# A gated linear attention kernel with a convolution-gated MLP: state updates of 48 columns, transposes of 112 rows, and a rewritten later part of the order

## The chip, the core and the metric

The kernel runs on one core of a Trainium2 chip. A core has five instruction queues that run side by side: PE (TensorE, matrix products, with its weight loads listed as PEld), DVE (VectorE), ACT (ScalarE), POOL (GpSimd) and SP (SyncE, which here only issues DMAs). The metric is the device time of one execution in microseconds (us). Before the change it is 304.14 us, the median of three runs (304.11 to 306.39).

## What is computed

Four sequences (b) of 768 steps with eight heads of 48 dimensions go through a gated linear recurrence. Its output goes through an MLP whose hidden layer is gated by a convolution over three neighbouring steps.

```
for t in range(S):                                # 768 steps
    state = f[:, :, t, :, None] * state + k_t (outer) v_t     # 48 x 48 for each head
    y[:, :, t] = q_t @ state
x = y of all heads side by side                   # 4 x 768 x 384
h = relu(x @ w_in)                                # 384 -> 1024
gate = sigmoid(conv_w[0]*h[t-1] + conv_w[1]*h[t] + conv_w[2]*h[t+1])
out = (h * gate) @ w_out                          # 1024 -> 384
```

All inputs are fp32, and f is the sigmoid of `f_logit`.

## The kernel before, in words

**Attention.** A sequence is cut into 6 chunks of 128 steps, so there are 24 chunks, numbered n = 0 to 23; c = n mod 6 is the chunk's place in its sequence. Heads are handled in four pairs p, the two heads j = 0, 1 of a pair in partitions 0 to 47 and 64 to 111. For each chunk, cumulative decays give `fi` and `fd`, by which k (on DVE, `scaled_k`) and q (mostly on POOL, `scaled_q`) are multiplied. Then:

- `turned` transposes k into a PSUM tile `ptk` (4 transposes of 128 by 128), and ACT copies 48 of each 64 columns to `kp`.
- `scores` makes the products of k and q in the PSUM tile `pa` (one tile for all chunks), and DVE copies the causal part into `am` under a mask (COPY_PREDICATED). There are two `am` tiles, used in turn.
- `values` makes `py` (one PSUM buffer): first from `am` and v, then, where a state exists, from the state `st` and q. ACT and then DVE move `py` to `xT`, split into a rounded high part and a low part.
- `state` makes k^T v in a PSUM tile `pk`. DVE adds the old state to it, and POOL multiplies the sum by the chunk's total decay `ft_all` into the next `st`. `last_decay` copies that decay from `fd` on POOL. Chunks with c = 5 have no `turned` and no `state`, so there are 20 of each. `ptk` and `pk` share one PSUM buffer in turn.

For n < 9 the state products use weights of 64 columns (two column halves of the array beside each other), from n = 9 on weights of 32 columns (four beside each other). Each moves 64 columns of v: 48 of its own head and 16 more, in reversed 32-column blocks for j = 1. A state row is 4 pairs by 64 columns = 256 columns wide.

**MLP.** A unit u is half a sequence (384 steps). `hidden` makes for each of 8 blocks f a PSUM tile `ph` from 9 products of 384 columns (high and low parts of weights and inputs, fp32r). ACT applies relu, then ACT and DVE make the convolution, `gated` applies tanh and the gate. `result` splits this into `gh` (ACT) and `gl` (DVE), makes a tile `po` of 128 steps from 24 products of 384 columns, and stores it. `ph`, `po` and some early tiles share three PSUM buffers.

**The order.** Nothing is scheduled automatically. The text ORDER names steps, and each name runs one more piece of that step's generator: F, V, L, M load f, v, k, q; x, G, p make the decays; t is `last_decay`; K and Q scale k and q; k is `turned`, a `scores`, s `state`, y `values`; h, m, j are the MLP's first part and r its second; I, J, H, O, P, S are weights; z counts the decays that are not too small and b loads that count into a register of every engine, for a branch to a slow path that is not taken here. Each engine runs its own pieces in the order in which they are written, so an instruction that waits holds up all that is behind it on its engine.

## Time and profile before

| | before |
|---|---|
| median of 3 runs | 304.14 us |
| the profiled execution's own span | 303.3 us |
| PE busy | 294.2 us, 97% of the span |
| PEld busy | 273.5 us, 90% |
| DVE busy | 251.3 us, 83% |
| ACT busy | 220.5 us, 73% |
| POOL busy | 85.3 us, 28% |
| granted TensorE clock | 1.00 of full speed throughout |

The profile is one execution. It lists for each engine when it was busy, groups instructions by their line, says what ended the idle time before an instruction, and follows the chain of work that ended last: 75% of that chain is PE, 31% in `po` and 28% in `ph`. Matrix products are pipelined: the start of one to the start of the next is the time that it really takes, while the duration shown includes a fixed latency.

### The profile page before, as it was taken

The numbers are of one execution on the slowest core, as the hardware profiler recorded it, in microseconds if no ns is written. First come the engines' busy times: TensorE is split into PE (matmuls) and PEld (weight loads), VectorE is DVE, ScalarE is ACT, GpSimd is POOL, SyncE is SP. The second block draws the span as 40 slices with busy tenths as digits, with TensorE's granted clock in tenths as the row PEclk, the third lists the DMA queues.
The fourth block names the chain that finished last, engine by engine and source line by source line (L and its number), as shares of the span: only waits on it lengthen the run. The fifth ranks groups of instructions, "written<-read, shape, count | busy, mean of one in ns | idle before, by whom it ended". The sixth has DMA issues, their size and how long they took to land.

```text
span 303.3 us, 8894 instructions
## 1 busy us (share of the span) xinstructions
PE 294.2 (97%) x3747; PEld 273.5 (90%) x3747; DVE 251.3 (83%) x380; ACT 220.5 (73%) x422; POOL 85.3 (28%) x107
## 2 busy tenths in 40 slices
PE   7799989999999999999999999999999999999994
PEld 5678878988999999999998999999999999999994
DVE  4999999999999999977999999946893976479520
ACT  4999979989967996767976995665756544676521
POOL 5475894344503140300323410230305010000000
PEclk9999999999999999999999999999999999999999
DMA  7999951194025411627315130602012000000211
GB/s 230 396 385 391 403 191 39 56 333 135 2 72 161 101 59 61 220 72 224 102 37 166 64 124 2 195 2 84 3 30 89 2 28 26 28 1 2 79 54 55
DMA packets 19374, 35.67 MB, mean 118 GB/s; under 512 B 2156, under 2 KB 9092, under 8 KB 19332
## 3 DMA queue, kind: packets, MB, share of 16 engines
q1 hardware_dynamic: 19044, 34.69, 33.8%
q8 instruction: 30, 0.49, 0.7%
q10 hardware_dynamic: 288, 0.39, 0.4%
q14 instruction: 12, 0.10, 0.1%
HBM read 30.35 MB, written 4.72 MB: 116 GB/s over the span
## 4 chain that ended last, share of the span: by engine, by line
PE 75%; DVE 7%; POOL 3%; issue 1%; ACT 1%; POOLq 0%
PE po L507 31%; PE ph L454 28%; PE py L398 8%; PE pa L351 3%; PE ptk L330 2%; DVE g L466 2%; PE pk L376 2%; DVE g L464 2%; DVE g L475 1%; POOL st L386 1%; PE pa L345 1%; DVE am L358 1%; PE pk L371 1%; POOL q L324 1%; DVE gl L495 1%
## 5 line engine op out<-in xcount | busy, mean ns | idle before, releaser
L454 PE MATMUL ph<-xT,wih 128*128 128x384 f32 x384 | 99.6, 340 | 0.0
L454 PEld LDWEIGHTS ph<-xT,wih 128*128 128x128 f32 x384 | 68.3, 188 | 1.0 <-issue 0.2
L507 PE MATMUL po<-woh,gh 128*128 128x384 f32 x192 | 64.7, 337 | 0.0
L454 PE MATMUL ph<-xT,wil 128*128 128x384 f32 x192 | 64.3, 335 | 0.0
L507 PE MATMUL po<-wol,gh 128*128 128x384 f32 x192 | 64.2, 334 | 0.0
L507 PE MATMUL po<-woh,gl 128*128 128x384 f32 x192 | 64.2, 334 | 0.0
L464 DVE SCALAR_TENSOR_TENSOR g<-hb,cw,g 128x384 f32<-128x384 f32 (+1 forms) x64 | 42.2, 667 | 13.0 <-ACT g L462 12.9
L466 DVE SCALAR_TENSOR_TENSOR g<-hb,cw,g 128x384 f32<-128x384 f32 (+1 forms) x64 | 40.5, 649 | 0.7
L457 ACT ACTIVATE hb<-ph 128x384 f32<-128x384 f32 x64 | 30.7, 487 | 11.4 <-PE ph L454 10.8
L495 DVE TENSOR_TENSOR gl<-g,gh 128x1024 fp32r<-128x1024 f32 (+4 forms) x34 | 30.4, 908 | 9.6 <-ACT gh L493 9.6
L462 ACT ACTIVATE g<-hb,cw 128x384 f32<-128x384 f32 (+1 forms) x64 | 38.0, 614 | 0.3
L507 PEld LDWEIGHTS po<-woh,gh 128*128 128x128 f32 x192 | 36.0, 188 | 0.5 <-issue 0.2
L324 POOL TENSOR_TENSOR q<-q,fd 128x512 f32<-128x512 f32 x19 | 26.9, 1419 | 33.0 <-ACT fd L307 24.3
L507 PEld LDWEIGHTS po<-wol,gh 128*128 128x128 f32 x192 | 36.0, 188 | 0.0
L507 PEld LDWEIGHTS po<-woh,gl 128*128 128x128 f32 x192 | 36.0, 188 | 0.0
L454 PEld LDWEIGHTS ph<-xT,wil 128*128 128x128 f32 x192 | 36.0, 188 | 0.0
L493 ACT CAST gh<-g 128x1024 fp32r<-128x1024 f32 (+4 forms) x34 | 26.4, 800 | 12.7 <-PE po L507 8.8
L386 POOL TENSOR_TENSOR st<-st,ft_all 128x256 f32<-128x256 f32 x16 | 20.8, 1301 | 51.7 <-DVE st L384 51.7
L475 DVE SCALAR_TENSOR_TENSOR g<-g,hb 128x768 f32<-128x768 f32 (+1 forms) x32 | 30.1, 952 | 3.7 <-ACT g L473 3.7
L512 ACT COPY ob<-po 128x384 f32<-128x384 f32 x24 | 11.3, 474 | 29.7 <-PE po L507 27.1
L473 ACT ACTIVATE g<-g 128x768 f32<-128x768 f32 (+1 forms) x32 | 26.7, 846 | 3.9 <-DVE g L466 3.8
L312 POOL COPY ft_all<-fd 128x4 f32<-128x4 f32 x24 | 12.7, 537 | 56.5 <-ACT fd L307 56.5
(92 smaller groups left out, 453.9 us busy)
## 6 DMA issues: line engine op xcount, KB each, us to landing
k<-in_k_dram SPq DMA_DIRECT2D x24, 256.0 KB, 4.4
q<-in_q_dram SPq DMA_DIRECT2D x24, 256.0 KB, 4.3
v<-in_v_dram SPq DMA_DIRECT2D x24, 224.0 KB, 4.3
fb<-in_f_logit_dram SPq DMA_DIRECT2D x18, 256.0 KB, 4.3
out_dram<-ob SPq DMA_DIRECT2D x22, 192.0 KB, 1.9
wis<-in_moe_w_in_dram SPq DMA_DIRECT2D x6, 512.0 KB, 6.0
wos<-in_moe_w_out_dram SPq DMA_DIRECT2D x8, 384.0 KB, 5.6
fb<-in_f_logit_dram SPq DMA_DIRECT2D x6, 200.0 KB, 4.9
```

Of the source, the lines that this page charges most:

```text
L324: (nc.vector if n < QV else nc.gpsimd).tensor_tensor(raw["q", n], raw["q", n], fds[n][1], ALU.mult)
L398: nc.tensor.matmul(py[G * p:G * p + G, t, :], lhs, rhs, start=start, stop=stop)
L454: nc.tensor.matmul(ph, w, xts[b, hf][:, t, xl, :], start=(k == 0), stop=(k == 3 * KT - 1))
L457: nc.scalar.activation(hb[:, 2:HS + 2], ph, AF.Relu, scale=0.5)
L462: nc.scalar.activation(cv, hb[:, 1:n + 1], AF.Copy, scale=cw[:, 1, f:f + 1])
L464: nc.vector.scalar_tensor_tensor(cv, hb[:, 2:n + 2], cw[:, 2, f:f + 1], cv, ALU.mult, ALU.add)
L466: nc.vector.scalar_tensor_tensor(cv, hb[:, 0:n], cw[:, 0, f:f + 1], cv, ALU.mult, ALU.add)
L473: nc.scalar.activation(cv, cv, AF.Tanh)
L475: nc.vector.scalar_tensor_tensor(cv, cv, 1.0, h_b[:, fp:fp + 2, 1:n + 1], ALU.add, ALU.mult)
L493: nc.scalar.copy(hi, g[:, f:f + k])
L495: nc.vector.tensor_tensor(lo, g[:, f:f + k], hi.bitcast(F32), ALU.subtract)
L507: nc.tensor.matmul(po, g[:, f, :], w, start=(i == 0), stop=(i == 3 * NF - 1))
```

## The change

1. `state` moves 48 columns in place of 64, those of its own head alone, now contiguous. To pack them, a state row becomes 288 columns: head 0 of pair p in columns 64p to 64p + 47 of the upper partitions, head 1 in columns 64p + 48 to 64p + 95 of the lower ones. The slices that `values` loads as weights start at multiples of 64 bytes, as before.
2. Between these parts lie columns that hold leftovers of the transposes. They are made zero by the decay: `ft_all` has a value for each 16 columns (18 of them, and 2 spare), is zero to begin with, and is filled by two POOL copies of 64 partitions by 4 by 3 in place of one of 128 by 4.
3. `turned` transposes 112 rows of k (both heads' rows) in place of 128, so 112 columns come out.
4. `ptk` and `pk` become one tile `sk` that is kept throughout. It is cleared once by DVE.
5. ORDER: the first 386 of its 1403 names are the same, up to about 80 us of the execution before; behind them the same names are written in another sequence.

```diff
-    s_b = [wk.tile([P, NP, HP], F32, name=f"st{i}", bufs=1) for i in range(2)]
+    s_b = [wk.tile([P, WS], F32, name=f"st{i}", bufs=1) for i in range(2)]
+    sk = ps.tile([P, NP, P], F32, name="sk")
+    pk = sk.rearrange("p n t -> p (n t)")[:, :WS]
+    nc.vector.memset(pk, 0.0)
-    ft_all = const.tile([P, B, NC, NP], F32, name="ft_all")
-    nc.gpsimd.memset(ft_all, 1.0)
+    ft_all = const.tile([P, B, NC, NU + 2], F32, name="ft_all")
+    nc.gpsimd.memset(ft_all, 0.0)
...
-        (nc.scalar.copy if n >= TS else nc.gpsimd.tensor_copy)(ft_all[:, b, c, :], fds[n][1][:, :, P - 1])
+        for j in range(2):
+            r, i0 = slice(HP * j, HP * j + HP), D // GAP * j
+            nc.gpsimd.tensor_copy(ft_all[r, b, c, i0:i0 + NP * HP // GAP].rearrange("p (n i) -> p n i", n=NP)[:, :, :D // GAP],
+                                  fds[n][1][r, :, P - 1:].broadcast_to([HP, NP, D // GAP]))
...
-            nc.tensor.transpose(pt[:, p, :], raw["k", n][:, p, :], ident)
+            nc.tensor.transpose(sk[:, p, :W2], raw["k", n][:W2, p, :], ident[:W2, :W2])
...
-                vv = vt[:, p, D * j:D * j + HP].rearrange("p (i e) -> p i e", e=G)
-                vv = vv[:, ::-1] if j else vv
+                vv = vt[:, p, HP * j:HP * j + D]
+                for x in (0,) if n < NA else (0, G):
+                    o, w = HP * j + x, HP if n < NA else G
+                    nc.tensor.matmul(pk[o:o + w, HP * p + D * j:HP * p + D * j + D], kp[:, 2 * p + j, x:x + w], vv,
                                      start=True, stop=True)
...
-k13 y11 k13 y11 a12 k12 K14 m2.0 m2.6 p15 m2.1 y11 m2.3 r0.2 r0.3 m2.3 m2.1 r0.4 r0.4 y11 m2.5 m2.4 M15 r0.4 r0.4 r0.4
+p12 k13 y10 s10 G14 m2.1 Q12 t12 M14 r0.2 L15 r0.5 r0.5 j2.4 m2.0 r0.4 k12 a12 y11 a12 y11 k12 y11 r0.5 Q13 a13 j2.4
+y11 V12 s12 y12 r0.4 m2.1 m3.4 m3.4 s12 m2.7 m3.0 m3.4 x15 h3.4 m2.2 m3.4 m2.0 m2.2 m2.0 j2.0 y12 j2.0 G17 j2.6 m3.0
```

With it go W2 = 112, WS = 288 and NU = 18.

**PE, the state products of chunk 22, before.** The row of `pk` stands first in a group of fp32 products between two stretches of the MLP (`ph`, `po`); the numbers in the names are the chunk's.

```order
L454 MATMUL ph6_2_3463<-xT3_0_2812,wil2_0_456 128x384
L376 MATMUL pk22_3503<-v22_3498,kp0_79 32x64 x16
L398 MATMUL py22_3520<-am0_75,v22_3498 32x128 x16
L398 MATMUL py22_3520<-q22_3032,st0_77 32x128 x12
L351 MATMUL pa_81<-q23_3306,k23_2428 64x128 x2
```

**PE, the same chunk in the change.** The stretch is cut between the repeating rows of `pa`.

```order
L338 MATMUL sk_82<-ident_88,k22_2638 128x112 x4
L359 MATMUL pa_81<-q22_3244,k22_2638 64x128 x2
...
L401 MATMUL py21_3383<-am1_76,v21_2457 32x128 x16
L401 MATMUL py21_3383<-q21_2597,st1_78 32x128 x12
L359 MATMUL pa_81<-q23_3197,k23_2824 64x128 x2
...
L378 MATMUL sk_82<-v22_2818,kp0_79 32x48 x16
L401 MATMUL py22_3461<-am0_75,v22_2818 32x128 x16
L401 MATMUL py22_3461<-q22_3244,st0_77 32x128 x12
```

The products are 48 and 112 columns wide. Two chunks now stand in one group: `pa` of chunks 22 and 23 with only `py` of chunk 21 between them, and `py` of chunks 21 and 22 with `pa` and the state products between them. Chunks 12 and 13 stand in the same way. Counted to the end of the fast path, PE goes from the MLP's products to fp32 products 24 times before and 22 times in the change.

**DVE, around the mask copy of chunk 22 in the change.** COPY_PREDICATED reads `pa`; g5 and g6 are gates of MLP units 5 and 6.

```order
L499 TENSOR_TENSOR gl2_2_3252<-g4_2485,gh2_2_3251 128x8x127
L479 SCALAR_TENSOR_TENSOR g5_2874<-g5_2874,hb_110 128x770 x2
L329 TENSOR_TENSOR k23_2824<-k23_2824,fi23_3246 128x2x128 x2
L468 SCALAR_TENSOR_TENSOR g6_3353<-hb_110,cw_116,g6_3353 128x384
L366 COPY_PREDICATED am0_75<-mask1_101,pa_81 128x1024
L432 TENSOR_TENSOR xT3_1_3420<-py21_3383,xT3_1_3420 128x3x128
```

Two gates, a k and a piece of convolution stand ahead of the copy, and the low part of `py` of chunk 21 behind it.

**POOL, some 30 us into the program, before.**

```order
L386 TENSOR_TENSOR st1_78<-st1_78,ft_all_110 128x256
L181 TENSOR_SCALAR mswo3_541<-mswo3_541 128x384
L312 COPY ft_all_110<-fd3_346 128x4
L312 COPY ft_all_110<-fd4_490 128x4
L179 TENSOR_SCALAR mswo0_607<-wos0_409 128x384
```

**POOL, the same place in the change.**

```order
L388 TENSOR_TENSOR st1_78<-st1_78,ft_all_112 128x288
L187 TENSOR_SCALAR mswo3_539<-mswo3_539 128x384
L320 COPY ft_all_112<-fd3_348 64x4x3 x2
L320 COPY ft_all_112<-fd4_489 64x4x3 x2
L185 TENSOR_SCALAR mswo0_607<-wos0_410 128x384
```

Each decay copy has become two, and the state product is 288 columns wide; the order is the same here.

## Rows read from the trace of the kernel before

**Rows 1.** The page's first part: engine, busy us, share of the span, instructions

```profile
PE 294.2 (97%) x3747; PEld 273.5 (90%) x3747; DVE 251.3 (83%) x380; ACT 220.5 (73%) x422; POOL 85.3 (28%) x107
```

**Rows 2.** Busy time by stretches: length, each engine's busy us, PEclk, DMA share, GB/s

```profile
75.00:100.00 25.00, 25.00 (x285) 24.07 (x287) 24.93 (x39) 19.60 (x36) 7.63 (x10) 1.00 0.24 71
200.00:225.00 25.00, 25.00 (x290) 24.16 (x277) 18.63 (x29) 15.67 (x30) 4.59 (x6) 1.00 0.08 26
```

**Rows 3.** A wait of PE's products: for whom, us in total, times, longest

```profile
PE py L398 <- POOL st L386: 1.1, 1, 1.1
```

**Rows 4.** PE's products by line and shape: weights, moving columns, count, busy us, mean ns

```profile
L398 PE MATMUL py<-am,v 128*32 128x128 f32 x768 | 25.8, 275 | 0.4 <-DVE xT L428 0.3
L330 PE MATMUL ptk<-ident,k 128*128 128x128 f32 x80 | 12.8, 282 | 0.1
L376 PE MATMUL pk<-v,kp 128*32 128x64 f32 x384 | 7.7, 221 | 0.0
```

**Rows 5.** Weight loads by line and shape, the same columns

```profile
L454 PEld LDWEIGHTS ph<-xT,wil 128*128 128x128 f32 x192 | 36.0, 188 | 0.0
L330 PEld LDWEIGHTS ptk<-ident,k 128*128 128x128 f32 x80 | 8.9, 140 | 2.0 <-DVE st L384 0.3 <-DVE cw L248 0.2 <-ACT kp L333 0.2
L376 PEld LDWEIGHTS pk<-v,kp 128*32 128x32 f32 x384 | 6.3, 110 | 1.8 <-issue 1.5 <-ACT g L462 0.2
L371 PEld LDWEIGHTS pk<-v,kp 128*64 128x64 f32 x128 | 4.5, 137 | 0.9 <-issue 0.2 <-ACT wos L185 0.2
```

**Rows 6.** PE in order of time: start us, length us, product; three stretches

```profile
63.65 0.34 PE L454 MATMUL ph<-xT,wil 128*128 128x384 f32 x1
63.92 0.69 PE L371 MATMUL pk<-v,kp 128*64 128x64 f32 x16
...
176.17 0.66 PE L330 MATMUL ptk<-ident,k 128*128 128x128 f32 x4
176.58 0.59 PE L454 MATMUL ph<-xT,wih 128*128 128x384 f32 x2
...
244.44 0.65 PE L376 MATMUL pk<-v,kp 128*32 128x64 f32 x32
244.91 1.06 PE L398 MATMUL py<-am,v 128*32 128x128 f32 x32
...
246.50 0.90 PE L351 MATMUL pa<-q,k 48*64 48x128 f32 x32
...
247.33 0.44 PE L507 MATMUL po<-woh,gh 128*128 128x384 f32 x1
247.61 0.34 PE L507 MATMUL po<-wol,gh 128*128 128x384 f32 x1
247.78 0.35 PE L507 MATMUL po<-woh,gl 128*128 128x384 f32 x1
```

**Rows 7.** POOL's decay copies: count, ns min/median/max, first and last start

```profile
L312 POOL COPY ft_all<-fd x24: 183/513/1833, 12.5 to 219.4; 128x4 f32<-128x4 f32 x24
```

**Rows 8.** POOL and DVE in order of time, 35 to 46 us

```profile
35.35 0.68 DVE L317 TENSOR_TENSOR k<-k,fi 128x512 f32<-128x512 f32 x1
...
39.08 4.27 POOL L386 TENSOR_TENSOR st<-st,ft_all 128x256 f32<-128x256 f32 x1
...
42.87 1.27 DVE L355 COPY_PREDICATED am<-mask,pa 128x1024 f32<-128x1024 uint8 x1
...
44.90 1.80 DVE L317 TENSOR_TENSOR k<-k,fi 128x512 f32<-128x512 f32 x1
```

**Rows 9.** ACT and DVE behind the last rows of Rows 6

```profile
246.67 0.48 ACT L426 CAST xT<-py 128x384 fp32r<-128x384 f32 x1 [0.47 <-PE py L398]
...
248.36 0.55 DVE L428 TENSOR_TENSOR xT<-py,xT 128x384 fp32r<-128x384 f32 x1
...
249.35 1.32 DVE L358 COPY_PREDICATED am<-mask,pa 128x1024 f32<-128x1024 uint8 x1
```

**Rows 10.** DMA issues: size of one, median us from issue to landing

```profile
q<-in_q_dram SPq DMA_DIRECT2D x24, 256.0 KB, 4.3
```

More of the change, by code (lines that the diff above doesn't have):

```diff
@@ new lines @@
+m7.6 m7.6 m7.6 m7.7 r2.3 r2.3 m7.6 m7.6 m7.6 j7.6 m7.3 m7.3 j6.4 m7.4 m7.4 r2.3 m7.2 r2.2 m7.4 r2.3 m7.5 m7.5 m7.5
+r3.0 h7.4 j7.6 r2.4 r2.4 r2.4 r2.4 m7.2 m7.3 m7.2 m7.4 m7.1 m7.4 m7.5 m7.5 r2.3 r2.5 r3.0 r3.0 r3.0 r3.0 r3.0 j7.2
+m7.0 m7.1 m7.5 r3.1 m7.0 m7.0 r3.1 m7.4 m7.5 m7.1 m7.4 j7.2 j7.0 j7.0 r3.0 r3.2 r3.2 r3.2 r3.2 r3.2 r3.2 r3.2 j7.4
+r3.2 r3.2 r3.2 r3.2 r3.1 r3.1 r3.1 j7.4 r3.1 r3.2 r3.2 r3.2 r3.2 r3.3 r3.1 r3.1 r2.4 r3.2 r3.2 r3.2 r3.0 r3.2 r3.2
+r3.3 r3.3 r3.3 r3.4 r3.3 r3.4 r3.3 r3.5 r3.3 r3.4 r3.4 r3.4 z b r3.3 r3.2 r2.4 r3.5 r3.5 r3.2 r3.5 r3.5 r3.4 r3.4 r3.4
@@ L79 @@
+r3.5 r3.5 r3.5
 """
@@ L108, in gla_moe_kernel @@
     G = 32
+    W2 = HP + D
+    WS = HP * (NP - 1) + 2 * D
+    NU = WS // GAP
     WHOLE = False
@@ L327, in turned @@
     def turned(n):
-        pt = ps.tile([P, NP, P], F32, tag="s", name=f"ptk{n}", bufs=SB)
         for p in range(NP):
-            nc.tensor.transpose(pt[:, p, :], raw["k", n][:, p, :], ident)
+            nc.tensor.transpose(sk[:, p, :W2], raw["k", n][:W2, p, :], ident[:W2, :W2])
         yield
@@ L333, in turned @@
         (nc.vector.tensor_copy if n >= KV else nc.scalar.copy)(
[L334 removed]
+            kps[n][:, :, :D], sk.rearrange("p n (j x) -> p (n j) x", j=2)[:, :, :D])
         yield
@@ L385, in state @@
             yield
-        (nc.gpsimd if c > 0 else nc.vector).tensor_tensor(new, add, ft, ALU.mult)
+        (nc.gpsimd if c > 0 else nc.vector).tensor_tensor(
+            new.rearrange("p (n e) -> p n e", e=GAP), add.rearrange("p (n e) -> p n e", e=GAP), ft, ALU.mult)
         yield
@@ L410, in values @@
             for p in range(NP):
-                product(p, 0, st[:, p, G:], qT[:, p, :])
+                product(p, 0, st[:, HP * p + G:HP * p + HP], qT[:, p, :])
             for p in range(NP):
@@ L414, in values @@
                     r = slice(HP * (t - 1), HP * (t - 1) + D)
-                    product(p, t, st[r, p, :G], qT[r, p, :], stop=True)
+                    o = HP * (p + t - 1)
+                    product(p, t, st[r, o:o + G], qT[r, p, :], stop=True)
             yield
@@ L536, in checked @@
     def checked():
-        ok = const.tile([P, n_ft], F32, name="ok")
-        nc.vector.tensor_scalar(ok, ft_all.rearrange("p b c n -> p (b c n)"), F_MIN, None, ALU.is_ge)
+        ok = const.tile([P, P], F32, name="ok")[:, :B * NC * (NP + 1)].rearrange("p (n i) -> p n i", i=NP + 1)
+        nc.vector.tensor_scalar(ok, ft_all.rearrange("p b c n -> p (b c) n")[:, :, :NU:HP // GAP], F_MIN, None, ALU.is_ge)
         yield
-        nc.vector.tensor_reduce(oks, ok, mybir.AxisListType.X, ALU.add)
+        nc.vector.tensor_reduce(oks, ok.rearrange("p n i -> p (n i)"), mybir.AxisListType.X, ALU.add)
         yield
-        pc = ps.tile([1, 1], F32, tag="s", name="pcnt", bufs=SB)
+        pc = sk[:1, 0, :1]
         nc.tensor.matmul(pc, oks, ones, start=True, stop=True)
```

108 lines of the change are left out of this document (46 added, 62 removed).

## Prediction

> **What bounds the kernel now.** I read the busy shares first, then the stretches, then PE's waits, then PE instruction by instruction. PE is busy in 97% of the span, DVE in 83% [rows 1]. By stretches PE is full from 75 us on, at a granted clock of 1.00, which is the 2.4 GHz level; DVE is as full up to 100 us (24.93 of 25) and has room later (18.63) [rows 2]. So a microsecond of work taken from PE is a microsecond of the end, as long as no other engine comes later than PE needs it. PE's waits say how close that is: apart from the start, the largest is one of 1.1 us for a state on POOL [rows 3], at 43 us; behind it no wait of its products reaches half a microsecond. What happens to PE's own work, and whether the new order still keeps PE from waiting, is all there is to price.
>
> **State products from chunk 9 on.** A block of 32 instructions begins at 244.44 and the next block at 244.91: 0.47 us [rows 6]. Four column parts run side by side, so that is 8 steps of some 56 to 59 ns. What sets a step is read from the products' lengths: 128 moving columns take 275 ns, 64 take 221 [rows 4], 54 ns for 64 columns or 0.84 ns a column, two clocks at 2.4 GHz. So 64 columns fill the step, and 48 save 16 x 0.84 = 13.5 ns. Weights don't stand in the way: loads of 32 columns take 110 ns and of 64 columns 137 [rows 5], again 0.84 ns a column, so 32 columns stream in 27 ns. The 384 instructions are 12 chunks x 8 steps x 4: 96 x 13.5 ns = **-1.30 us**.
>
> The Trainium skill (TensorE: Matmul & The Clock Gate, section Back-to-back issue gap) gives all products of 1 to 64 columns one gap, about 60 cycles. By it 48 columns would cost what 64 do, this term would be 0 and the sum 1.3 us worse. The trace speaks against it here: four instructions share 56 to 59 ns.
>
> **State products before chunk 9.** Their weights are 64 columns wide, and these stream in 64 x 0.84 = 54 ns, as long as the 64 moving columns did. With 48 the load stays and sets the step. Bounds: 0, and 8 chunks x 8 steps x 13.5 ns = -0.86. I take **-0.1**, nearer to the load's row.
>
> **Transposes.** Four take 0.41 us (176.17 to 176.58) [rows 6]. 112 columns in place of 128 save 13.5 ns each if the moving columns set the pace, nothing if the load of 128 weight columns does. A transpose's load is shorter (140 ns) than that of the MLP, as wide (188) [rows 5]. With the fixed part of 83 ns (110 less 27) it streams for 57 ns, well below the 103 ns between two. So the columns set it: 80 x 13.5 ns = **-1.08**. Bounds 0 and -1.08.
>
> **Visits to fp32 products.** Going in costs 0.10 us (63.65 to 63.92 is 0.27, an MLP product takes 0.17: 247.61 to 247.78), coming out 0.11 (247.33 to 247.61 is 0.28) [rows 6]. The order has 22 visits in place of 24: 2 x 0.21 = **-0.42**. All other products are the same.
>
> That makes -2.90 us for PE.
>
> **What is added, on POOL and DVE.** 24 more decay copies of 0.18 to 1.83 us, median 0.51 [rows 7]; 16 state products wider by an eighth; the adds on DVE by some 0.05 us each, and one clearing of a PSUM tile while DVE waits for the first inputs. None of it is on PE. Behind 100 us POOL has 20 of 25 us free and DVE 6 [rows 2], and the copies cost nothing. Before 80 us there are 10 of them beside a full DVE. The worst place is the one POOL wait: that state product took 4.27 us, from 39.08 to 43.35, and ended only when DVE came to a copy out of PSUM at 42.87 [rows 8]. A copy ahead of it delays its start by half a microsecond or more, but hardly its end, since DVE holds it up anyway. That cover gone, the wait of 1.1 us would grow by the copies' length. The other way round, a k product on DVE took 1.80 us beside POOL's work and 0.68 at another time [rows 8], so a copy costs DVE between 0 and 1.1 us, all ten 0 to 11. PE has stalled little in this stretch, so DVE stands mostly ahead of it; part of that room goes, and some of the PE time saved early can't be used. I take **+0.4**.
>
> **What is moved.** Two places of the new order are tighter than anything before; the rows of chunks 21 to 23 show one, 12 and 13 are the other. (1) The second `pa` must wait until DVE has copied the first. Between them stands only `py`, 244.91 to 246.50 = 1.59 us [rows 6]; the copy takes 1.32 [rows 9], and a semaphore each way some 0.2. That just fits if DVE stands ready. Behind that `pa` wait the state products and the next `py`. (2) The second `py` needs the first to be taken out of its only buffer: ACT started 0.17 us behind `py` and took 0.48, DVE takes 0.55 [rows 9], so some 1.4 with handovers. Cover: `pa` 0.83 (246.50 to 247.33) and the state products 0.36, together 1.2 [rows 6]. That is short by 0.2 or 0.3 even with DVE and ACT ready. I take 0.25 for each place, **+0.5** for both. The upper bound is DVE as late as in the trace: there the mask copy began at 249.35, 2.0 us behind the end of `pa` at 247.33, and DVE's part of `py` 1.2 us behind ACT's end [rows 6, 9]. Then `pa` would wait 2.0 + 1.3 - 1.6 = 1.7 and `py` some 0.5 more: 2.2 for a place, 4.4 for both.
>
> Loads are moved too, on SP's queue. The tightest is q of chunk 17: its buffer is free behind `py` of chunk 15, some 10.4 us of PE's work (60 products of 0.173) ahead of `pa` 17. The load takes 4.3 us [rows 10] and POOL's product 1.4; behind it on POOL stands q of chunk 18, wanted later. It is hidden with some 4 us to spare. The end is alike: 72 products of other tiles still cover the last unit's convolution. The last count of decays now comes to DVE late, ahead of one `gl`, well before PE needs that. Both cost 0.
>
> **Sum.** -2.90 + 0.4 + 0.5 = -2.0. The profiled span is 303.3 us, the median run 304.14, 0.8 around and beside it, which stays: 301.3 on the first scale, **302.1** on that of the runs. What a measurement of this kernel can tell from no change is about 1%, 3 us: faster is below 301.1, slower above 307.2.
>
> **Rivals.**
> - *The order is clean.* DVE and ACT stand ready, early room suffices: -2.90, or -3.7 with the early state products in full: 301.2 to 300.4, mostly faster. For it: PE waits nearly nowhere now. Against it: 1.2 us of cover for 1.4.
> - *DVE is late at the two double places.* +4.4 in place of +0.5: 306.0. For it: DVE was 2.0 us late in the row. Against it: it has 6 us of 25 free there, and is late where nobody waits.
> - *Narrower products are not shorter*, the change doesn't do what it says, as by the skill's section above: only -0.42, so 304.6. Against it: the column's price from two pairs of rows.
> - *Slower: POOL's copies hold up DVE early.* With 1.1 us for each of ten, all passed on to PE: -2.9 + 11 + 0.5 = +8.6, 312.7. It decides from about 0.55 us a copy. The skill (GPSIMD Engine Reference, section Specifications) states the mechanism: GpSimd shares its SBUF interfaces with VectorE and contends with instructions of two SBUF inputs. The trace agrees, with 4.27 us on POOL and 1.80 on DVE. Against it: 14 such copies stand before 80 us now, and PE hardly waits.
>
> **How the numbers follow.** Forecast 0.47 (its own range 301.1 to 303.3), clean order 0.25, DVE late 0.13, no shorter products 0.08, POOL and DVE 0.07. From 300.4, the clean end, to 304.8, above the unshortened products, lie the forecast, nearly all of the clean order and of the third rival, and the milder half of a late DVE: 0.83. Faster: the clean order and the forecast's edge, 0.28. Slower: the POOL rival and a sliver of late DVE, 0.08. Same: 0.64.
>
> **What would show it.** State blocks of 0.36 us from chunk 9 on and 0.6 before; four transposes in 0.36 us and not 0.41; PE busy about 3 us shorter. New waits of PE for the mask copy and for `py` at chunks 12 and 22 and nowhere else, each below 0.5 us. At 43 us still one wait of about 1.1 us for POOL. I am wrong if PE's waits behind 100 us sum to over 1.5 us, if waits for DVE grow between 20 and 80 us, or if block lengths haven't moved.

## The result

The changed kernel takes 308.45 us (median of four runs, 308.05 to 308.79) beside 304.61 us for the kernel before in the same comparison: a ratio of 1.0117, interval 1.0084 to 1.0149, so 3.6 us slower. The forecast was 302.1 with a range of 300.4 to 304.8. The result lies outside of it, on the other side of no change.

| | before | after |
|---|---|---|
| span of the profiled execution | 303.3 us | 306.4 us |
| from the first product's start to the last one's end on PE | 298.2 us | 301.2 us |
| DVE busy | 251.3 us | 253.4 us |
| ACT busy | 220.5 us | 223.5 us |
| POOL busy | 85.3 us | 90.7 us |
| share of PE in the chain that ended last | 75% | 45% |

The page's busy line of after answers to [rows 1], and below it stands the line on the chain of work that ended last, by engine:

```profile
PE 294.9 (96%) x3747; PEld 273.5 (89%) x3747; DVE 253.4 (83%) x381; ACT 223.5 (73%) x424; POOL 90.7 (30%) x131
...
PE 45%; DVE 30%; ACT 5%; issue 3%; DMA 2%; POOL 1%; SPq 0%; DVEq 0%; ACTq 0%
```

PE is as busy as before and not 3 us less, and DVE, with 7% of that chain before, now has 30%. ACT has two instructions more (424 in place of 422) and 3 us more.

**What was saved.** PE's products of the changed shapes in after (weights, moving columns, count, busy us, mean ns), to be read beside [rows 4]:

```profile
L338 PE MATMUL sk<-ident,k 112*128 112x112 f32 x80 | 11.6, 267 | 0.4 <-DVE st L388 0.4
...
L378 PE MATMUL sk<-v,kp 128*32 128x48 f32 x384 | 6.5, 208 | 0.0
L378 PE MATMUL sk<-v,kp 128*64 128x48 f32 x128 | 5.3, 225 | 0.7 <-ACT hb L439 0.7
```

And PE in order of time, to be read beside [rows 6] (start us, length us, product):

```profile
205.38 0.61 PE L338 MATMUL sk<-ident,k 112*128 112x112 f32 x4
205.76 0.42 PE L511 MATMUL po<-woh,gh 128*128 128x384 f32 x1
...
215.59 0.55 PE L378 MATMUL sk<-v,kp 128*32 128x48 f32 x32
215.96 1.06 PE L401 MATMUL py<-am,v 128*32 128x128 f32 x32
```

A state product is 13 ns shorter (221 to 208), and a block of 32 takes 0.37 us to the next block where it took 0.47. Four transposes take 0.38 in place of 0.41. These savings are there.

**What was lost.** PE's waits in after (for whom, us in total, times, longest), of which the first two belong to the start:

```profile
PE pl L298 <- ACT fb L277: 2.1, 2, 1.4
PE pw L177 <- POOL st L137: 1.3, 1, 1.3
PE py L401 <- DVE xT L432: 0.7, 2, 0.4
PE sk L378 <- ACT hb L439: 0.7, 1, 0.7
PE po L511 <- ACT hb L461: 0.6, 1, 0.6
PE pa L359 <- POOL q L333: 0.6, 2, 0.5
```

The wait of 1.1 us for the state on POOL [rows 3] is gone, and many small ones for three engines have come. That is one half. The other half doesn't show as a wait. The last 168 products of `po` are one stretch in which nothing waits, and the two lines below, from the chains of before and of after (start us, length us), compare it:

```profile
270.27 29.14 PE po L507 x168
```

```profile
273.01 29.51 PE po L511 x168
```

The same products take 0.37 us longer: 2.2 ns each on average. The granted clock is 1.00 over both stretches. From start to start, groups of three MLP products (two with a high part of the weights, one with a low part) take 520 ns before and 527 after (medians), in `ph` and in `po`, over the whole span as in its last 70 us. The code of these products isn't changed, nor are their operands.

So two things had to be explained: slower products without a wait (1152 of them, at 2.2 ns 2.5 us), and new waits.

### The profile page after: what moved, and what is told of

The parts are those of the page before. It is cut to its first block, busy times and chain, and to the rows that moved or that the text cites. A ratio compares the mean times of both kernels' runs of the same rounds, so it can differ in the third digit from the quotient of the medians.

```text
span 306.4 us, 8929 instructions
## 1 busy us (share of the span) xinstructions
PE 294.9 (96%) x3747; PEld 273.5 (89%) x3747; DVE 253.4 (83%) x381; ACT 223.5 (73%) x424; POOL 90.7 (30%) x131
## 4 chain that ended last, share of the span: by engine, by line
PE 45%; DVE 30%; ACT 5%; issue 3%; DMA 2%; POOL 1%; SPq 0%; DVEq 0%; ACTq 0%
PE po L511 23%; PE ph L458 14%; PE py L401 4%; DVE g L470 4%; DVE g L468 4%; DVE g L479 4%; DVE gl L499 3%; DVE fb L303 3%; DVE am L366 3%; PE pa L359 2%; DVE k L329 2%; DMA fb<-in_f_logit_dram 2%; PE sk L378 1%; DVE am L363 1%; DVE xT L432 1%
## 5 line engine op out<-in xcount | busy, mean ns | idle before, releaser
L458 PEld LDWEIGHTS ph<-xT,wih 128*128 128x128 f32 x384 | 69.0, 188 | 2.5 <-issue 1.0
L511 PE MATMUL po<-woh,gh 128*128 128x384 f32 x192 | 66.3, 345 | 0.6 <-ACT hb L461 0.6
L511 PE MATMUL po<-woh,gl 128*128 128x384 f32 x192 | 64.9, 338 | 0.0
L468 DVE SCALAR_TENSOR_TENSOR g<-hb,cw,g 128x384 f32<-128x384 f32 (+1 forms) x64 | 38.4, 615 | 10.0 <-ACT g L466 10.0
L470 DVE SCALAR_TENSOR_TENSOR g<-hb,cw,g 128x384 f32<-128x384 f32 (+1 forms) x64 | 40.8, 662 | 0.5
L479 DVE SCALAR_TENSOR_TENSOR g<-g,hb 128x768 f32<-128x768 f32 (+1 forms) x32 | 32.0, 1014 | 10.8 <-ACT g L477 10.8
L499 DVE TENSOR_TENSOR gl<-g,gh 128x1024 fp32r<-128x1024 f32 (+4 forms) x34 | 32.2, 959 | 9.1 <-ACT gh L497 9.1
L388 POOL TENSOR_TENSOR st<-st,ft_all 128x288 f32<-128x288 f32 x16 | 13.9, 870 | 63.1 <-DVE st L386 62.7
L320 POOL COPY ft_all<-fd 64x12 f32<-64x12 f32 x48 | 22.3, 465 | 34.7 <-ACT fd L313 33.1
L401 PE MATMUL py<-am,v 128*32 128x128 f32 x768 | 25.8, 275 | 1.0 <-DVE xT L432 0.7
```

The lines of the kernel that those rows point to most:

```text
L401: nc.tensor.matmul(py[G * p:G * p + G, t, :], lhs, rhs, start=start, stop=stop)
L458: nc.tensor.matmul(ph, w, xts[b, hf][:, t, xl, :], start=(k == 0), stop=(k == 3 * KT - 1))
L468: nc.vector.scalar_tensor_tensor(cv, hb[:, 2:n + 2], cw[:, 2, f:f + 1], cv, ALU.mult, ALU.add)
L470: nc.vector.scalar_tensor_tensor(cv, hb[:, 0:n], cw[:, 0, f:f + 1], cv, ALU.mult, ALU.add)
L479: nc.vector.scalar_tensor_tensor(cv, cv, 1.0, h_b[:, fp:fp + 2, 1:n + 1], ALU.add, ALU.mult)
L499: nc.vector.tensor_tensor(lo, g[:, f:f + k], hi.bitcast(F32), ALU.subtract)
```

## The experiments

Each run has its own comparison with the kernel before, on one chip. "Ratio" is this run to before, with its interval.

| run | low weights start at (mod 512 bytes) | order | products | us | ratio (interval) | group of three |
|---|---|---|---|---|---|---|
| after | 128 | new | narrow | 308.45 | 1.0117 (1.0084 to 1.0149) | 527 |
| x3_after_512 | 0 | new | narrow | 306.61 | 1.0064 (1.0047 to 1.0081) | 520 |
| x1_old_order | 128 | old | narrow | 305.71 | 1.0029 (1.0002 to 1.0057) | 527 |
| x5_old_order_512 | 0 | old | narrow | 304.13 | 0.9995 (0.9966 to 1.0025) | 520 |
| x4_before_128 | 128 | old | wide | 306.69 | 1.0076 (1.0047 to 1.0106) | 527 |
| x2_new_order | 0 | new | wide | 305.53 | 1.0005 (0.9981 to 1.0029) | 520 |

"Narrow" stands for 48 columns, 112 rows and two decay copies, "wide" for what before has. "Group of three" is the median time in ns from the start of one group of three MLP products to the start of the next.

### Where the tiles lie

The change makes `ft_all` 1536 bytes longer in each partition, `ok` 128, and each state tile 128. All that is allocated behind them moves: the low parts of the MLP weights (`wil`, `wol`) start at a multiple of 512 bytes before and 128 bytes past one after; `xT`, `gh` and `gl` go from 0 to 384 past one. The high parts (`wih`, `woh`) stay at a multiple of 512.

**x3_after_512**

```diff
-        ok = const.tile([P, P], F32, name="ok")[:, :B * NC * (NP + 1)]...
+        ok = const.tile([P, P + 96], F32, name="ok")[:, :B * NC * (NP + 1)]...
-    s_b = [wk.tile([P, WS], F32, name=f"st{i}", bufs=1) for i in range(2)]
+    s_b = [wk.tile([P, 384], F32, name=f"st{i}", bufs=1)[:, :WS] for i in range(2)]
```

> The changed kernel with 384 bytes added to one constant and 384 to each of the two state tiles, so that the MLP weights, the activations and the state lie at multiples of 512 bytes again as in the kernel before. Theory C (where a tile starts sets the period of the MLP products: 527 ns a group of three after, 520 before): 384 groups x 7 ns = 2.7 us less, 305.8, groups at 520 ns. Rival (the 7 ns come from something else, such as other traffic at the time): 308.4, groups at 527 ns.

Measured: 306.61 us, 1.8 less than after (1.6 by the ratios), and groups at 520 ns. Its last 168 products of `po` (the chain, as above):

```profile
270.91 29.14 PE po L511 x168
```

**x4_before_128**

```diff
-        ok = const.tile([P, n_ft], F32, name="ok")
+        ok = const.tile([P, n_ft + 32], F32, name="ok")[:, :n_ft]
-    s_b = [wk.tile([P, NP, HP], F32, ...) for i in range(2)]
+    s_b = [wk.tile([P, NP * HP + 32], F32, ...)[:, :NP * HP].rearrange("p (n e) -> p n e", e=HP) for i in range(2)]
```

> The kernel before with 128 bytes added to one constant and 128 to each of the state tiles, and nothing else: weights, loads and state at 128 bytes past a multiple of 512, activations at 384 past, as after. Theory C (places in memory): 304.6 + 2.7 = 307.3, groups of three at 527 ns. Rival: 304.6, groups at 520 ns.

Measured: 306.69 us, 1.9 more than the 304.82 of its comparison, groups at 527 ns, and the same tail as after:

```profile
271.61 29.51 PE po L507 x168
```

Not one instruction differs from the kernel before. The place alone costs 1.9 us by the medians (2.3 by the ratio, interval 1.4 to 3.2). Giving it back gains 1.6 us in the changed kernel (after to x3_after_512) and 1.0 with the old order (x1_old_order to x5_old_order_512), both by the ratios. Theory C holds. The time is the less sure part: three of the four runs of x4_before_128 have a granted clock of 0.993 or 0.994 (in the profiled one it is 0.50, the level of 1.2 GHz, from 8.3 to 11.6 us, where the kernel before has 1.00). PE's products show the place by themselves: from the 60th MLP product, at 47 us, to the last, this run falls 2.3 us behind the kernel before, 2.1 ns a product. The time shows less than the 2.5 us of 1152 x 2.2 ns because the POOL wait of 1.1 us at 43 us is gone in this run as well (see the last section).

**x9_weights_0 and x10_acts_0** tell which tiles it is. Each is the changed kernel with one of the two pads.

```diff
# x9_weights_0
-        ok = const.tile([P, P], F32, name="ok")...
+        ok = const.tile([P, P + 96], F32, name="ok")...
# x10_acts_0
-    s_b = [wk.tile([P, WS], F32, ...) for i in range(2)]
+    s_b = [wk.tile([P, WS + 32 - 32 * i], F32, ...)[:, :WS] for i in range(2)]
```

> The changed kernel with 384 bytes added to one constant only: the low parts of the MLP weights at multiples of 512 bytes, the activations (xT, gh, gl) at 256 past one. If the place of the weights sets the period: groups of three MLP products at 520 ns in both products. If that of the activations does: 527, unless 256 counts as well placed.

> The changed kernel with 128 bytes added to one state tile only: the activations at multiples of 512 bytes, the low parts of the weights at 128 past one. If the place of the weights sets the period: 527 ns. If that of the activations does: 520 ns. If the moving operand alone counts: 520 in the first MLP product (xT moves), 527 in the second (the weights move).

The same 30 products of `ph` and 168 of `po` in the chains of both, first x9, then x10:

```profile
260.10 5.20 PE ph L458 x30
...
271.54 29.14 PE po L511 x168
```

```profile
260.29 5.27 PE ph L458 x30
...
271.88 29.51 PE po L511 x168
```

With the low weights at 0 and the activations at 256 both products are fast; with the weights at 128 and the activations at 0 both are slow. So it is the place of the weights, whether they are the stationary operand (in `ph`) or the moving one (in `po`). One run each gave 306.27 and 306.98 us.

**z3_weights_256 and z4_weights_64** try two more places, with narrow products in the old order: `ok` is `[P, P + 32]` and `[P, P + 112]`, and the state tiles are padded as in x5_old_order_512. The activations move along: they lie at 256 and 64 as well.

> The widths in the old order with the low parts of the weights (and what lies behind them) at 256 past a multiple of 512 bytes. If a multiple of 256 is enough: groups of three MLP products at 520 ns, if it takes 512: at 527 or near it.

> As the run before, at 64 past a multiple of 512 bytes. If the cost goes with the place in a line of 64, 128 or 256 bytes: more than 527 ns if 64 is worse than 128, 527 if any place but the good ones costs the same.

At 256 all groups take 520 ns (305.76 us in one run). At 64 the two products part. The rows of the chain for 72 `ph` and 168 `po`, first x5_old_order_512 (at 0), then z4_weights_64:

```profile
255.81 12.48 PE ph L458 x72
268.29 29.14 PE po L511 x168
```

```profile
257.24 12.64 PE ph L458 x72
269.88 29.13 PE po L511 x168
```

`ph` loses 2.2 ns a product again, `po` nothing (304.71 us in one run). So 0 and 256 are free in both products, 128 costs in both, and 64 in `ph` alone, where the low weights are stationary. Whether at 64 it is the weights or `xT`, the moving operand there, that slows `ph` stays open, since both moved and no run has them apart at 64. It isn't a matter of size: 64 is no worse than 128. Nor is it the clock, since one execution has slow `ph` and fast `po`, both at a granted 1.00.

### The order and the widths, apart

**x1_old_order and x5_old_order_512** are the changed kernel, and the changed kernel at multiples of 512 bytes, with the ORDER of before. **x2_new_order** is the kernel before with the ORDER of after. The names in both orders are the same, so the text is exchanged and nothing else.

> The changed kernel with the written order of before: the widths (48 columns, 112 rows, two decay copies) without the moves. Theory A, the new order makes TensorE wait for DVE, ACT and POOL: its waits (about 4.4 us of new gaps in the trace after) go, the 1.1 us wait for the POOL state product comes back, so 308.45 - 4.4 + 1.3 = about 305.4. Theory B, the waits come from the 24 additional decay copies on POOL, and the order is harmless: 308 to 309, gaps at 22, 101 and 145 us stay. In both the three MLP products stay at 527 ns per group, since the places in memory are those of after.

> The changed kernel with the tiles at multiples of 512 bytes again and with the written order of before: the widths alone. If places and order are the two causes and independent: 306.6 (places mended) - 2.7 (what the old order gave at the shifted places) = 303.9, or 0.9 us under the kernel before; the widths' own -1.3 (state) -0.8 (transposes) give 302.7 less whatever the earlier arrival at 40 to 75 us loses again. Rival (the order only costs because the products are slower): 306 to 306.6.

> The kernel before with the written order of after and none of the widths. Theory A (order): 304.6 + 4.4 - 1.3 = about 307.7, with gaps of TensorE near 22, 101 and 145 us. Theory B (the widths bring the waits): within 1 us of 304.6.

With narrow products the old order takes back 2.7 us at the places of after (1.0117 to 1.0029) and 2.1 at the good ones (1.0064 to 0.9995), near what theory A said for both. Its rival, that the waits come from the additional copies and the order is harmless, falls with x1: the copies are in it. But x2 missed: I expected 307.7, and the new order with wide products costs 0.05% with an interval of 0.24% to either side. By the ratios, order and widths don't add: alone, each is about neutral; together they cost 2 us. How sure that is: the 2.0 us come from three ratios whose intervals together are worth some 1.3 us to either side. In the profiled executions the order alone isn't neutral: from the 120th MLP product, at 69 us, to the last, PE's stream in x2_new_order is 1.6 us longer than in the kernel before, and in x3_after_512 2.7 us longer than in x5_old_order_512. So the surplus of the two together is 1 to 2 us, and that the order costs nothing alone isn't shown.

The next table shows where. It adds up, over stretches of the profiled execution (for x2 the slowest of its ten runs, for x5 the fastest of its twelve), what each of PE's starts comes later than that succession of products usually takes (the 30th percentile over these runs), in us:

| stretch | before | x2 (order) | x5 (widths) | x3 (both) | after |
|---|---|---|---|---|---|
| 75 to 90 us | 0.22 | 0.22 | 0.22 | 0.48 | 0.37 |
| 90 to 110 us | 0.11 | 0.30 | 0.11 | 1.23 | 1.07 |
| 110 to 130 us | 0.25 | 1.49 | 0.62 | 0.62 | 0.52 |
| 130 to 160 us | 0.59 | 1.05 | 0.57 | 1.66 | 1.62 |
| 160 to 200 us | 0.58 | 0.44 | 0.90 | 0.75 | 0.87 |
| 240 to 260 us | 1.26 | 0.59 | 1.26 | 0.65 | 0.67 |

Between 75 and 160 us both columns of the new order have waits that the old order hasn't: 3.1 us with wide products in place of 1.2, and 4.0 with narrow ones in place of 1.5. Behind 240 us the new order gives 0.6 back, and two fewer visits to fp32 products 0.4. That leaves 0.8 for the order alone and 1.4 with the narrow products, and the times say the same within their error; PE's whole stream says 1.6 and 2.7, as above, so the table misses about a microsecond in each. My reading of the difference, not tested by itself: in the new order PE meets what it waits for no sooner when its own products get shorter, so part of what they save is waited away.

What moved in the order shows in the sequence of PE's blocks. From chunk 11 on the new order puts the scores (`pa`) of many chunks ahead of the state and value products of the chunk before. So q on POOL and k on DVE are wanted about 2 us sooner. Around 101 us in after (scores of chunk 11):

```profile
97.00 1.77 POOL L320 COPY ft_all<-fd 64x12 f32<-64x12 f32 x2 [14.19 <-ACT fd L313]
...
98.86 0.68 POOL L388 TENSOR_TENSOR st<-st,ft_all 128x288 f32<-128x288 f32 x1
...
99.49 1.29 POOL L333 TENSOR_TENSOR q<-q,fd 128x512 f32<-128x512 f32 x1
...
100.83 0.57 PE L359 MATMUL pa<-q,k 48*64 48x128 f32 x16 [0.46 <-POOL q L333]
```

POOL goes from the two decay copies through the state to q without a pause, and the scores start 0.5 us later than they usually follow an MLP product. At 145 us it is a load:

```profile
137.85 0.34 SPq L518 DMA_DIRECT2D out_dram<-ob  x1
...
138.73 0.43 SPq L265 DMA_DIRECT2D fb<-in_f_logit_dram  x1
...
143.41 1.49 ACT L274 ACTIVATE fb<-fb 128x1536 f32<-128x1536 f32 x1 [1.91 <-DMA fb<-in_f_logit_dram]
...
144.88 0.48 ACT L461 ACTIVATE hb<-ph 128x384 f32<-128x384 f32 x1
...
145.42 0.44 PE L511 MATMUL po<-woh,gh 128*128 128x384 f32 x1 [0.64 <-ACT hb L461]
```

The load of f for chunk 20 stands two names ahead of the exponential that reads it, and on SP's queue behind a store that waited until 137.85. ACT waits 1.9 us for it, then relu comes late, then `po`.

### Which part of the new order costs

All runs of this part have the narrow products and good places (base x3_after_512, 306.61 us, unless said otherwise).

**x6_new_then_old and x7_old_then_new** change from one order to the other at the 345th MLP product, about 125 us.

> As the run before (multiples of 512), but the new order up to the 345th MLP product (about 125 us), and what is left in the old order from there. Theory: of the order's 2.7 us the trace after has 0.15 + 0.8 + 0.3 = 1.3 us before 130 us, so 1.3 us above the widths alone, about 305.2; waits at 100 and 117 us are there, those at 145 and 178 us not. Rival (one load and its exponential at 139 to 145 us are the whole of it): as the widths alone, 303.9.

> As the run before with the halves swapped: the old order up to the 345th MLP product and the new one behind. Theory: 1.05 + 0.1 us of waits between 130 and 200 us, 0.6 us given back at 240 to 260 us: 0.5 us above the widths alone, about 304.4, with a wait of near 0.8 us at 145 us behind the load of the gate logits for chunks 15 to 17. Rival (the moves before 125 us are harmless, those behind are the cost): 306.

Measured 309.76 us (1.0148, interval 1.0092 to 1.0204) and 323.61 us (1.0640, 1.0581 to 1.0700). Both miss by far. The seams cost more than the halves, above all 5.5 us ahead of the scores at 126 us and 5.0 us ahead of `po` at 144 us in x7, where loads and steps that the first order leaves for later are wanted at once. The granted clock fell there too: at three waits of PE of over 2 us in x7 (at 126, 144 and 162 us) and at one in x6 (135 us) it went to 0.50, the level of 1.2 GHz, and MLP products took 0.32 us in place of 0.17. In x7 17 us are at the lower level, worth some 7 of the 19 us lost (an estimate from the parts of them that lie behind the waits). Of use is one thing: x6 has the new order's waits before 130 us as they were (start-to-start times of 0.61 us at 95, 0.87 at 101, 0.52 at 117 us, beside 0.60, 0.85 and 0.54 in the base). They are made by the early part.

**x8_one_copy**

```diff
-        for j in range(2):
+        for j in range(1 if n >= NA else 2):
```

(and four small memsets of `ft_all` at the start; from chunk 9 on the kernel leaves out the decay of the odd heads, which stays at 1)

> The changed kernel at multiples of 512 bytes in its new order, but from chunk 9 on only one of the two decay copies on POOL; the odd heads' decays are set to 1 at the start instead, so that their state is not the reference's. Theory (the second copy stands in POOL's chain ahead of q at 100 and 117 us): 0.5 us less at each, 305.6. Rival (POOL has room, the waits are the order's alone): 306.6.

Measured: 310.48 us (1.0202, 1.0144 to 1.0260; the two of its four runs at a granted clock of 0.999 or more 309.24 and 309.36), slower than the base. The wait at 101 us did get shorter by 0.37 us, by about one copy. The one at 117 us grew by 1.0. POOL and DVE there, first in the base, then in x8:

```profile
113.46 1.70 POOL L320 COPY ft_all<-fd 64x12 f32<-64x12 f32 x2
...
114.51 0.59 DVE L468 SCALAR_TENSOR_TENSOR g<-hb,cw,g 128x384 f32<-128x384 f32 x1
...
115.23 1.29 POOL L333 TENSOR_TENSOR q<-q,fd 128x512 f32<-128x512 f32 x1
```

```profile
113.83 1.12 POOL L322 COPY ft_all<-fd 64x12 f32<-64x12 f32 x1
...
114.88 1.74 DVE L470 SCALAR_TENSOR_TENSOR g<-hb,cw,g 128x384 f32<-128x384 f32 x1
...
114.91 1.29 POOL L335 TENSOR_TENSOR q<-q,fd 128x512 f32<-128x512 f32 x1
```

Without the second copy POOL's q begins as DVE's product does, and DVE's product takes 1.74 us and not 0.59; the mask copy behind it is late, and the scores with it. A step less on POOL made DVE later. The Trainium skill (SBUF — State Buffer, section SBUF: two separate sides) states that a VectorE instruction with two SBUF inputs and a GpSimd instruction that reads SBUF take a shared port in turn, each for its whole length; the two pairs of rows agree, with 1.15 us more beside an instruction of 1.29. (DVE's row begins 0.03 us ahead of POOL's, so which of the two goes first can't be read from the starts.) What the second copy costs over the whole kernel isn't told by this run: it has further waits of 0.8 and 1.6 us at 133 and 149 us that I haven't traced.

**y1_x15 and y2_x15_x18**

```diff
# y1: the second x15 goes 26 names ahead
-... r0.5 r0.5 j2.4 m2.0 ... m3.0 m3.4 x15 h3.4 ...
+... r0.5 r0.5 x15 j2.4 m2.0 ... m3.0 m3.4 h3.4 ...
# y2: besides, the first x18 goes 17 names back
-... F20 M19 x18 h3.2 m3.3 ... s13 r1.1 y13 r1.0 ...
+... F20 M19 h3.2 m3.3 ... s13 r1.1 y13 x18 r1.0 ...
```

> The changed kernel at multiples of 512 bytes, with one item of the new order put back: the logarithm of the gates of chunks 15 to 17 (x15, second step) ahead of the tanh of j2.4, as the old order has it. The traces show 10 table loads of 1.28 us on ACT with the new order and 8 with the old one, and the two additional ones at 113 and 118 us stand between these two items. Theory (ACT's 2.6 us there delay what TensorE waits for at 117 us and behind): 8 table loads, 0.4 to 1 us less than the 306.6 of this base. Rival (ACT has room there, the waits are DVE's and POOL's): 8 table loads, 306.6 as before.

> The run before, and in addition the exponential of the gates of chunks 18 to 20 (x18, first step) 17 items later, so that ACT no longer stands behind a load issued 2 items ahead of it (1.9 us idle at 141 us in the trace after, 1.1 in that of the base). Theory: 0.5 to 0.8 us less than the run before. Rival (the wait near 145 us is for DVE's masked copy and POOL's q, behind other loads): no change.

Measured: 306.86 us (1.0063, 1.0020 to 1.0106) and 308.41 us (1.0105, 1.0066 to 1.0144). In y1 the table loads fall from 10 to 8 and the time doesn't move, as the rival said. That ACT's 2.6 us cost nothing isn't shown by it: the move brings two waits at 119 us, for `kp` on ACT and `xT` on DVE, 1.1 us together, while those at 137 and 146 us shrink by 0.65. In y2 the wait at 145 us is gone, but one of 1.2 us for the state on DVE has come at 151 us, and the run is slower by about 1.5 us. Mending one late step makes the next one late.

**z1_new_scores_back and z2_old_scores_early**

```diff
# z1, new order: the first a11, a13 and a15 go back
-... a11 ... y10 ... y10 ...            +... y10 ... y10 a11 ...
-... Q13 a13 ... s12 y12 ... y12 ...    +... Q13 ... s12 y12 ... a13 y12 ...
-... a15 ... y14 y14 ...                +... y14 y14 a15 ...
# z2, old order at multiples of 512: the first a11 and a15 go ahead
-... s10 y10 y10 a11 ...                +... a11 s10 y10 y10 ...
-... s14 y14 y14 ... a15 ...            +... a15 s14 y14 y14 ...
```

> The changed kernel at multiples of 512 bytes and in its new order, but the score products of chunks 11, 13 and 15 stand again behind the state and value products of the chunk before (13: one value group and 12 MLP products later), as in the old order. Theory (the order costs because it asks for the scores some 2 us earlier, when POOL's q and DVE's mask are not there): the waits ahead of the scores at 101 (0.65 us), 117 (0.35) and 145 us (0.4 to 0.6) go, 1.4 us less than the 306.6 of this base: 305.2. Rival (the chain that feeds the scores is late anyway, and the wait only moves to the next product): 306 to 306.6, waits of DVE, POOL and ACT of the same sum at other products.

> The run with the old order at multiples of 512 bytes (304.1), with the score products of chunks 11 and 15 alone moved ahead of the state and value products of the chunk before, as the new order has them. Theory: a wait of 0.6 us for POOL's q ahead of the scores near 100 us and one of 0.4 to 0.6 us near 143 us, so 305.1. Rival (the move is harmless by itself): 304.1, no new wait.

Measured: z1 307.06 us (1.0067, 1.0037 to 1.0097), nothing gained: the waits at the three scores are gone, and others have come at 104, 119 and 147 us (for DVE's `xT` and ACT's `hb`). z2 306.62 us (1.0042, 1.0012 to 1.0072): moving two scores ahead costs the old order 1.4 us by the ratios. That is no sure size, since six of its ten runs have a granted clock of 0.987 to 0.993 and take 306.61 to 307.70 us; the other four take 304.83 to 305.96, where x5's eight runs above 0.996 take 303.01 to 304.42. From the 120th MLP product on PE's stream is 1.3 us longer than in x5. The one new wait is at 101 us:

```profile
100.44 0.75 DVE L329 TENSOR_TENSOR k<-k,fi 128x256 f32<-128x256 f32 x2
...
100.95 1.06 PE L359 MATMUL pa<-q,k 48*64 48x128 f32 x32 [1.63 <-issue]
```

The scores begin 0.5 us after DVE has begun k of chunk 11 (two instructions, 0.75 us together), and POOL's q, which the theory named, was done at 97.70. In x5 they come at 100.79 too, but with the state and value products of chunk 10 ahead of them. At 143 us nothing happened, against the theory. So scores put early can be a cost where DVE is late; but in the new order they aren't what the cost hangs on, as the rival of z1 says.

**w1_new_less_dve and w2_old_less_dve** leave out one of DVE's three pieces of the convolution in token groups 1 to 3.

```diff
-            nc.vector.scalar_tensor_tensor(cv, hb[:, 0:n], cw[:, 0, f:f + 1], cv, ALU.mult, ALU.add)
+            if u not in (1, 2, 3):
+                nc.vector.scalar_tensor_tensor(cv, hb[:, 0:n], cw[:, 0, f:f + 1], cv, ALU.mult, ALU.add)
```

> The changed kernel at multiples of 512 bytes in its new order, with the last product of the convolution (line 470, 24 instructions of about 0.6 us on DVE) left out in the token groups 1 to 3, which DVE does between 76 and 170 us; the output is not the reference's. DVE is 98% busy in this base from 14 to 110 us and 96% from 130 to 160. Theory (the new order's waits are all DVE's lateness, whichever engine is named): waits between 90 and 160 us fall from 3.5 to under 1 us, 304.1. Rival (POOL, ACT or loads are late by themselves): 306 to 306.6.

> The same instructions left out in the run with the old order (304.1). Theory: that order has hardly a wait behind 75 us, so it gains at most 0.5 us: 303.6 to 304.1, and what is left between the two orders is under 1 us, where it was 2.5. Rival: both gain alike, and 2 to 2.5 us stay between them.

Busy time in three stretches (length, then PE, PEld, DVE, ACT, POOL), first the base, then w1:

```profile
90.00:110.00 20.00, 19.22 (x214) 18.10 (x213) 19.65 (x31) 16.91 (x30) 4.33 (x5) 1.00 0.23 77
110.00:130.00 20.00, 19.73 (x274) 18.65 (x273) 18.45 (x27) 17.44 (x28) 5.62 (x6) 1.00 0.23 74
130.00:160.00 30.00, 29.44 (x483) 26.82 (x482) 28.93 (x41) 23.73 (x41) 9.35 (x14) 1.00 0.38 121
```

```profile
90.00:110.00 20.00, 20.00 (x220) 19.27 (x219) 16.61 (x25) 18.10 (x33) 3.29 (x5) 1.00 0.23 77
110.00:130.00 20.00, 20.00 (x276) 18.98 (x276) 15.39 (x20) 17.16 (x29) 5.73 (x7) 1.00 0.24 78
130.00:160.00 30.00, 29.54 (x483) 26.80 (x482) 23.53 (x31) 23.83 (x41) 8.93 (x13) 1.00 0.37 122
```

With DVE at 16 of 20 us PE has no idle time left between 90 and 130 us: the waits at 95, 101 and 117 us are all gone, those put down to POOL and ACT too. w1 takes 305.05 us (1.0016, 0.9993 to 1.0040), 1.5 us less than the base, and the waits of these two stretches are 1.4 us less (0.4 in place of 1.85). So these waits were DVE's lateness. Between 130 and 160 us nothing changed (29.54 beside 29.44), though DVE has 6 us free: there it is something else. POOL's q still waits for its load there, and PE ahead of the scores of chunk 15. POOL, then PE, of w1 in order of time:

```profile
141.23 2.19 POOL L333 TENSOR_TENSOR q<-q,fd 128x512 f32<-128x512 f32 x1 [2.50 <-DMA q<-in_q_dram]
```

```profile
145.37 0.90 PE L359 MATMUL pa<-q,k 48*64 48x128 f32 x32 [0.33 <-issue]
```


w2 went against the theory: 303.45 us (0.9953, 0.9917 to 0.9989), a gain of 0.7 us (1.3 by the ratios) where I allowed 0.5. So what stays between the orders is 1.6 to 1.9 us and not under 1. Its execution spends 0.5 us less in waits between 160 and 200 us; the rest I can't place.

What is shown, then: the new order with the narrow products costs 2 to 2.7 us, and with the wide ones 0.2 by the ratio and 1.6 in the profiled execution. Of the former about 1.4 us are waits at 95 to 117 us, which vanish when DVE has less to do. What is only read from the traces: that the rest, near 1 us at 136 to 146 us, comes from loads that stand late on SP's queue. It is open why the old order gains from less DVE work too, and so how much of the difference is DVE's in the end.

No run that does the whole computation beats the kernel before beyond its error. The best, x5_old_order_512, is the widths alone, with good places and the old order, at 304.13 beside 304.48 us.

## Why the forecast failed, step by step

- **State products from chunk 9 on, -1.30:** right. A block takes 364 ns in place of 470 (medians of start to start), 12 x 106 = 1.27 us.
- **State products before chunk 9, -0.1:** right, 615 to 602 ns, 8 x 13 = 0.1. The weights that stay set the step, as the row of their loads said.
- **Transposes, -1.08:** the mechanism was right, the size not. Four take 372 ns in place of 412. That is 40 ns and not 54: three steps of 13.5 ns and not four. The likely reason, not tested, is that the last of the four is followed by another product, which sets that step. 20 x 40 = -0.8.
- **Visits, -0.42:** nothing in the traces speaks against it; the blocks of PE show the 24 and 22.
- **"All other products are the same":** this step failed. The 1152 MLP products cost 2.2 ns more each, because the low weights, which lie behind `ft_all` and `ok`, had moved to 128 bytes past a multiple of 512. I had read in the diff that `ft_all` and the states grew, and had priced what they cost POOL, but not that everything behind them moves. +2.5 us on PE, 1.0 to 1.9 in the time of three pairs of runs.
- **POOL and DVE early, +0.4:** near in size by luck; the mechanism was wrong. x1 and x4 differ in the widths alone (the places and the order are the same). Up to the 120th MLP product, at 69 us, x1 loses 0.5 us; from there to the end it gains 1.5. But the wait of 1.1 us at 43 us that I said would stay is gone, and not in after alone: in all 17 traces with narrow products the state product on POOL takes 0.67 or 0.68 us and not 4.27. In its place DVE is late between 50 and 70 us in after, for `xT` at 53 us (0.5), for the state at 60 (0.4) and for `xT` at 67 (0.35), 1.3 us together. The rival on POOL counted 14 decay copies before 80 us; the trace of before has 10.
- **Two double places, +0.5:** right there. In after the scores of chunk 13 wait 0.24 us and the second `py` behind them 0.1 (the state block ahead of it takes 452 and not 364 ns); at chunks 22 and 23 the scores don't wait, and the second `py` again 0.1. Together 0.45.
- **What else is moved, 0:** this step failed too. I looked for tight places by their cover on PE and took the two tightest. The other waits are at places with more cover: the `ph` at 95 us (0.3), scores at 101 us (0.5), `po` at 145 us (0.8), a `py` at 178 us (0.3). There the suppliers were late, not the cover short. [rows 2] had DVE at 24.93 of 25 us up to 100 us; I used that for the copies alone. And I took DVE's 6 free us from the row of 200 to 225 us for everything behind 100 us; two stretches between have DVE with 23.84 and 24.37 of 25 us (the rows below). For a step moved ahead into such a stretch it means that its operands come no sooner. And I tested SP's queue at chunk 17 alone, while f of chunk 20 had come to stand two names ahead of its use. DVE is the third busy time in these rows of the kernel before:

```profile
100.00:125.00 25.00, 25.00 (x380) 23.41 (x369) 23.84 (x36) 21.73 (x38) 4.73 (x5) 1.00 0.37 109
...
150.00:175.00 25.00, 24.88 (x390) 22.90 (x391) 24.37 (x35) 20.74 (x36) 9.19 (x8) 1.00 0.25 81
```

- **The sum:** by the measured terms -1.3 - 0.1 - 0.8 - 0.4 + 2.5 + 0.45, and 1.9 for the other waits (0.3 + 0.5 + 0.8 + 0.3), is +2.25. The early part adds 1.3 for the three waits for DVE, takes off 1.3 for the POOL wait (start to start), and the MLP begins 0.5 later: +2.75. The last MLP product starts 3.1 us later; 0.35 is left unplaced.
- **The rivals:** "narrower products are not shorter" is refuted by the block lengths, and the rule of the Trainium skill behind it (TensorE: Matmul & The Clock Gate, section Back-to-back issue gap: one gap from 1 to 64 columns) doesn't hold for four products side by side: 8 steps of 59 ns became 8 of 46. "POOL's copies hold up DVE early" is no cause: with those copies and the old order the time is that of before (x5). "DVE late at the double places" had the right engine and the wrong places. None of the rivals had the places in memory, and none had a cost that comes of order and widths together. My own sign that I am wrong, PE's waits behind 100 us of over 1.5 us, came true: the places named in the two bullets above the sum come to 2.35 us, of which 2.05 lie behind 100 us. So did the second, waits for DVE that grow between 20 and 80 us.

## What to carry to other kernels

When a change makes a tile larger or smaller, compare the addresses of all tiles allocated behind it, above all of those that a long run of products reads: here 128 bytes cost PE 2.5 us, more than the narrower products gave it (2.2), and a pad takes it back. Where an engine is full over a stretch, time saved on another engine in that stretch turns into waits, and a step that is moved ahead in it meets operands that come no sooner; price a new order by when its operands arrive, not by the cover on the engine that waits. And run the parts of such a change one by one, since their costs need not add: here the order cost 2 to 2.7 us with the narrow products and 0.2 to 1.6 with the wide ones.

## What the runs showed of the hardware

- The mean period of 384-column fp32r products with 128 x 128 weights, in runs of two with a high and one with a low part of the weights, depends on where the low weights start: 173.5 ns at 0 and 256 past a multiple of 512 bytes, 175.7 at 128, in both products (29.14 and 29.51 us for the same 168). At 64 past, with the activations at 64 too, it is 175.6 where the low weights are the stationary operand (12.64 for 72) and 173.4 where they move (29.13 for 168). The place of the activations at 0, 256 and 384 made no difference. Why, no run here shows.
- One POOL instruction, the state product at 39 us, takes 4.27 us in the kernel before [rows 8] and 0.61 in x4_before_128, whose instructions are the same. Both times it begins 0.04 or 0.05 us ahead of the same DVE instruction: in before that one takes 0.54 us, and POOL ends 0.48 us behind the start of DVE's copy out of PSUM, six DVE instructions on; in x4 that one takes 0.99 us. With the long one goes the wait of 1.1 us [rows 3]. It is long in before and x2_new_order (wide, low weights at 0) and in no other of the 20 traces; whether the place or chance makes it short in x4 isn't told by one trace.
- Executions of the same instructions at the same places can differ by 0.8 us before 70 us: in y1_x15, the same as x3_after_512 up to there, a relu on ACT comes 0.9 us late at 39 us, and in x3 not. It does so in eight of the 17 traces with narrow products, so a difference of this size between two profiled spans says little.
- A load of ACT's tables takes 1.28 us; there are 8 with the old order and 10 with the new. The run without the two more (y1) is no faster, but has other waits.
